# Later operand sums, no w_q checks beside the first products, more checks in the last blocks, and another order of part products

## The chip, the cores and the metric

The kernel runs on one core of one Trainium2 chip. The metric is the device time of one execution in microseconds (us), median of several executions. Five engines work side by side, each through its own instructions in a fixed order: TensorE (PE, matrix products), VectorE (DVE), ScalarE (ACT), GpSimd (POOL) and SyncE (SP, which here issues nearly all transfers between the chip's memory and the core).

## The reference

For x of 2048 tokens by 512 numbers, the output is x plus two branches of the layer-normed x, called xn here.

```python
# branch A: real part of a 2-D Fourier transform
a = einsum("bsd,ed->bse", xn, dft_hid_re); b = einsum("bsd,ed->bse", xn, dft_hid_im)
y = einsum("ts,bse->bte", dft_seq_re, a) - einsum("ts,bse->bte", dft_seq_im, b)
# branch B: 32 heads of product-key experts
q = einsum("nd,dhc->nhc", xf, w_q); q1, q2 = q[..., :128], q[..., 128:]
s1 = einsum("nhd,ed->nhe", q1, k1); s2 = einsum("nhd,ed->nhe", q2, k2)
i1, i2 = the 2 best of 64 in s1, s2; t1, t2 = their scores
cand = t1[:, None] + t2[None, :]; eidx = i1 * 64 + i2      # 2 x 2 candidates
top_s, top_e = the 2 best candidates; g = softmax(top_s)
act = gelu(einsum("nd,nhkd->nhk", xf, u[top_e]))           # u, v: 4096 x 512
out = einsum("nhk,nhk,nhkd->nd", g, act, v[top_e])
```

## The kernel before

The tokens are 16 blocks of 128. Branch A takes the first 116 us and is not touched. Branch B is `part_b`, in two halves.

**Scores.** There are 128 steps: 8 chunks of heads by 16 token blocks. A step is 12 products on PE (`s_mm`, L252) into one bank of PSUM, a scaled copy to SBUF by ACT (L951, tiles `ss<chunk>_<block>`, four buffers), and on DVE a search for the best two of 64 for each head (MAX8 L955, FIND_INDEX8 L959). After the last block of a chunk its routing (L884 to L924: candidate sums, softmax weights `g`, packed indices `z`) is done by POOL, DVE and ACT in pieces set beside later steps. A list, `todo`, names the other work of each step. To it belong: `fill_uv` (ACT L780 and L781, POOL L782), which splits a 512 KB piece of u or v into a rounded half-precision part and the rest; `sum_u` and `sum_x`, which make the sums of operands that a Strassen-like product needs. `sum_x(b, part)` serves the pair of token blocks b, b+1. Its part 0 runs on POOL (L822 to L831: a copy of one element that orders it behind a score step, one 1024-wide subtraction L823, four 256-wide sums), its part 1 splits the result (`split4`: ACT L794, POOL L795), its part 2 stores it. As scratch it borrows two neighbouring v tiles, `v<n>` and `v<n+1>`, before those are filled with v itself. The six pairs begin at blocks 2, 4, 6, 8, 10 and 12.

**Products.** Then come 16 `z` stages (x times u, all 4096 experts, gelu) and 16 `v` stages (masked weights times v). The order is written out in `phases`: z0, z1, v0; six rounds of a z pair (b, b+1), v(b-1), v(b); then z14, v13, z15, v14, v15. A stage has 8 column groups, a pair 16. A single z stage runs a column group as 48 products (L1095) into one of four banks, which ACT empties with the gelu (L1102). A pair runs 8 of its 16 groups plainly, `c` in the order below, two blocks to a product, and the other 8 in two quads, `a` and `b`, with seven products in place of eight: `1a` is operation 1 of quad a. Each operation takes 24 products (L1164); results stay in banks X, Y and Z until all parts are added, and ACT and DVE carry the parts (L1191 to L1214). X of a quad is freed by the gelu L1191 that follows operation 4.

Beside the products the weights of the next block are built: `g_mm` (G; DVE L1242, L1247 and L1250 make one-hot masks L and R, PE L1252 multiplies them) and `w_part` (W; DVE L1260 takes gelu output times g from PSUM, ACT L1267 rounds it to a half, DVE L1268 keeps the rest).

Third, the kernel checks itself: 68 units `U` compare stored transform matrices with inputs (`compare`, `compare_w`: one load, several DVE operations, an ACT sum of magnitudes L1373 or L1418), 35 units `F[0]` are `fit` on w_q or on v pieces that are not resident (a 512 KB load at L1424 or 256 KB at L1431, then a sum of magnitudes on ACT at L1425 or L1432), and units `F[1]` do the same on resident pieces (L1436). All of these tiles and the w tiles of W turn in one pool tag, `"w"`, with four buffers. `step` runs a unit: first it issues the ACT sums that are waiting, all but the newest, then the next unit's load.

`put(phase, column group, ...)` fills the table `plan`, which says what runs behind which column group. These lines are what the change rewrites:

```python
for ph in phases[:3]:                          # z0, z1, v0
    for cg in range(1, 9, 2):
        put(ph, cg, F[0])
for ph in phases[3:]:
    if ph[0] == "z":
        for cg in (8,) if len(ph) == 3 else (1, 4):
            put(ph, cg, F[0])
        for cg in range(7, 17, 2) if len(ph) == 3 else ():
            put(ph, cg, U)
```

A list scheduler turns the program into a fixed order for each engine from its own estimates of durations, so an edit at one place moves the neighbours too.

Of the kernel before, what the change touches and what calls it, by code (L numbers as in the profile page):

```python
# [29 lines left out]
V1 = 5  # L30
# [6 lines left out]
def tile_fnet_peer(ctx, tc, x, ca, cb, c5, wt, wf, wr, wq, kt, ut, vn, out):  # L37
# [683 lines left out]
    def part_b(safe, stS, stP, stQ, stE, xt, u_sb, cmp_p, w4):  # L721
# [93 lines left out]

        def sum_x(b, part, at=None):

            n = (0, 2, 4, 4, 7, 5)[PAIRS.index(b)]
            f, t4 = scratch(n), scratch(n + 1)
            if part == 0:  # L820
                v = xq[b // 2]
                nc.gpsimd.tensor_copy(f[:, 0:1], behind(one, at))  # L822
                nc.gpsimd.tensor_tensor(f.rearrange("p (q f) -> p q f", q=2),  # L823
                                        v[:, :, 0].rearrange("p q k n -> p q (k n)"),
                                        v[:, :, 1].rearrange("p q k n -> p q (k n)"), op=ALU.add)
                b11, b21, b12, b22 = [f[:, k * 256:k * 256 + 256] for k in range(4)]
                r = [t4[:, k * 256:k * 256 + 256] for k in range(4)]
                nc.gpsimd.tensor_tensor(r[0], b12, b11, op=ALU.subtract)
                nc.gpsimd.tensor_tensor(r[1], b22, r[0], op=ALU.subtract)
                nc.gpsimd.tensor_tensor(r[2], b22, b12, op=ALU.subtract)  # L830
                nc.gpsimd.tensor_tensor(r[3], b21, r[1], op=ALU.subtract)  # L831
                return
            split4(part - 1, t4, f.bitcast(F16)[:, 0:2 * D],
                   lambda i: t_d[b // 2, :, i * 2 * D:i * 2 * D + 2 * D], at)
# [154 lines left out]
        fills = [divmod(n, 16) for n in (0, 1, 2, 8, 3, 10, 16, 4, 12, 14, 17, 5, 9, 11, 18, 6, 13, 15, 19, 7, 20,  # L989
                                         21, 22, 23, 24)]  # L990
        slots = [29, 31, 36, 43, 45] + [16 * j + i for j in range(3, 7) for i in (4, 6, 11, 13)]
        slots += [115 + 2 * n for n in range(len(fills) - len(slots))]
        assert fills[slots.index(115)] == (1, V1)
        for (which, g), n in zip(fills, slots):
            todo[n].append(lambda at, w=which, g=g: fill_uv(w, g, at))
            todo[n - (3 if n < 115 else 1)].append(lambda at, w=which, g=g: fill_load(w, g))
            if which == 0 and not safe and any(g in q for q in QUADS):
                todo[n + 5].append(lambda at, g=g: (sum_u(g, 1, at), sum_u(g, 2)))
        if not safe:
            for n, b in zip((19, 22, 25, 102, 106, 108), PAIRS):  # L1000
                todo[n].append(lambda at, b=b: sum_x(b, 0, at))
                todo[n + 5].append(lambda at, b=b: (sum_x(b, 1, at), sum_x(b, 2)))
        for g, n in zip(range(V2, 16), (25, 38, 41, 57, 73, 89, 105)):
            todo[n].append(lambda at, g=g: stage_v(g, at, False))
            todo[n - 3].append(lambda at, g=g: fill_load(1, g))
# [98 lines left out]
        if not safe:  # L1104
            sx = stE.enter_context(tc.tile_pool(name="sx", bufs=1, side="left"))
            x4 = sx.tile([P, 2, 4, 2, P], F16, name="x4")
            PLAIN = [g for g in range(16) if not any(g in q for q in QUADS)]
            SEQ = [o if o == "c" else o + q for q in "ab" for o in "152c6c3c7c4"]
            OPS = {"1": (0, None, None, 0), "2": (1, None, None, 1), "5": (None, 0, 0, None), "6": (None, 1, 1, None),
                   "3": (None, 3, None, 3), "7": (None, 2, 2, None), "4": (3, None, 3, None)}  # L1110

# [59 lines left out]
        def z_pair(b, n, after):  # L1171

            cgs = iter(PLAIN)
            st = {}
            total, done, cg = sum(2616 if o == "c" else 1344 for o in SEQ), 0, 0
            for o in SEQ:
                if o == "c":
                    u_part(b, next(cgs))
                    done += 2616
                else:  # L1180
                    op, qd = o[0], ("ab".index(o[1]) + n) % 2
                    quad = QUADS[qd]

                    def dst(a, c):
                        return ACT[b[c]][:, 2 * quad[0] + a:2 * quad[3] + 2:2 * (quad[1] - quad[0]), :]

                    def v(p):
                        return p.rearrange("p (t n) -> p t n", t=4)

                    def gelu(d, src=None):  # L1190
                        nc.scalar.activation(d, d if src is None else src, AF.Gelu_apprx_tanh, scale=zsc)  # L1191

                    if op in "125":
                        st["X" if op == "1" else "Y" if op == "2" else "Z"] = take(f"z{op}_{b[0]}_{qd}")
                    (X, Xt), (Y, Yt), (Z, Zt) = [st.get(k, (None, None)) for k in "XYZ"]
                    slot(op, quad, Z if op in "53" else Y if op == "2" else X, qd)
                    if op == "1":
                        nc.scalar.activation(dst(0, 0), v(X), AF.Copy)
                    elif op == "2":
                        nc.vector.tensor_tensor(dst(0, 0), v(Y), dst(0, 0), op=ALU.add)  # L1200
                        banks.append(Yt)
                    elif op == "5":
                        nc.scalar.activation(dst(1, 0), v(Z), AF.Copy)
                    elif op == "6":
                        nc.scalar.activation(dst(0, 1), v(X), AF.Copy)
                        gelu(dst(0, 0))
                    elif op == "3":
                        nc.vector.tensor_tensor(dst(0, 1), v(Z), dst(0, 1), op=ALU.add)
                        banks.append(Zt)
                    elif op == "7":  # L1210
                        nc.scalar.activation(dst(1, 1), v(X), AF.Copy)
                        nc.vector.tensor_tensor(dst(1, 1), dst(1, 1), dst(1, 0), op=ALU.add)
                        gelu(dst(0, 1))
                    else:  # L1214
                        gelu(dst(1, 0), v(X))
                        gelu(dst(1, 1))
                        banks.append(Xt)
                    done += 1344
                while cg < 16 and done * 16 >= (cg + 1) * total:
                    after(cg)  # L1220
                    cg += 1
# [276 lines left out]
        def take(name):  # L1498
            tag = banks.pop(0)
            return psz.tile([P, 512], F32, tag=tag, name=name), tag  # L1500
# [56 lines left out]
        for b in range(14):  # L1557
            put(("v", b), 3, lambda b=b: compact_d(b + 2))
        if not safe:
            for ph in phases[:3]:  # L1560
                for cg in range(1, 9, 2):
                    put(ph, cg, F[0])
            for ph in phases[3:]:
                if ph[0] == "z":
                    for cg in (8,) if len(ph) == 3 else (1, 4):
                        put(ph, cg, F[0])
                    for cg in range(7, 17, 2) if len(ph) == 3 else ():
                        put(ph, cg, U)
                elif ph[1] < 14:
                    for cg, f in enumerate((None, F[1], F[1], None, U, U, U, F[0]) if ph[1] % 2 == 0 else (  # L1570
# [2 lines left out]
                            put(ph, cg, f)  # L1573
            for cg in range(3):
                put(("v", 14), cg, F[1])
                put(("v", 15), cg, F[1])
            for f, n in ((U, 68), (F[0], NK + 16 - V2), (F[1], 16 + V2)):
                assert sum(v.count(f) for v in plan.values()) >= n
# [188 lines left out]
```

## Time and profile before

| what | value |
|---|---|
| median of 3 runs | 1156.5 us (1153.89 to 1159.17) |
| the profiled execution, its own time | 1156.79 us |
| its span in the trace | 1154.7 us |
| PE busy | 1123.6 us, 97% of the span |
| DVE busy | 952.2 us, 82% |
| ACT busy | 642.1 us, 56% |
| POOL busy | 314.5 us, 27% |
| mean granted TensorE clock | 0.994 of full |

The span is what the trace covers; the 2.1 us between it and the execution's time lie outside the trace. The stages stand in the trace so: branch A up to 116 us, scores up to 419.69, z0 to 443.8, z1 to 480.86, v0 after it, the pairs from about 500 to 1031, then z14, v13, z15, v14 and v15; the last product ends at 1147.9. Timeline rows read: start, duration, engine, line, operation, output<-input with shapes, how many in a row, and in brackets the idle time of that engine just before, with what ended it. A waits row reads: engine and line that waited <- what ended the wait: us in total, times, longest.

### The profile page before, as it was taken

How to read it: one execution, taken by the hardware profiler on the slowest of the kernel's cores; microseconds unless marked ns; L12 is line 12 of the kernel's file. 1: busy time of each engine (PE TensorE's matmuls, PEld its weight loads, DVE VectorE, ACT ScalarE, POOL GpSimd, SP SyncE). 2: the span in 40 equal slices, each digit the busy share in tenths (PEclk: the TensorE clock that was granted, in tenths of full speed). 3: DMA queues.
4: the chain of work that ended last, by engine and by line, in shares of the span. 5: the costliest groups of instructions: out<-in, count | busy, mean ns of one | idle time of the engine just before them, and what ended most of it. 6: DMA issues, size and time to landing. Idle time of an engine off the chain costs nothing.

```text
span 1154.7 us, 27307 instructions
## 1 busy us (share of the span) xinstructions
PE 1123.6 (97%) x10748; PEld 726.8 (63%) x10748; DVE 952.2 (82%) x2855; ACT 642.1 (56%) x1086; POOL 314.5 (27%) x342
## 2 busy tenths in 40 slices
PE   9999999999999896999999999999999999999997
PEld 6455554544544366769579479569569568658763
DVE  7899979989888896894996897898987887888570
ACT  6557598788786554555436535535535535533440
POOL 1425996788789710000010010010010010000000
PEclk9999999999999999899999999999999999999999
DMA  9983554534433206663764664654665655452423
GB/s 290 289 208 137 169 193 153 172 102 164 158 98 111 92 15 237 208 242 106 238 203 154 224 206 175 226 198 169 223 204 185 222 193 196 156 175 73 130 74 104
DMA packets 114856, 198.36 MB, mean 172 GB/s; under 512 B 34068, under 2 KB 57499, under 8 KB 114718
## 3 DMA queue, kind: packets, MB, share of 16 engines
q1 hardware_dynamic: 114416, 196.45, 51.0%
q8 instruction: 86, 1.41, 0.5%
q14 instruction: 52, 0.43, 0.1%
q10 hardware_dynamic: 302, 0.08, 0.0%
HBM read 165.75 MB, written 24.97 MB: 165 GB/s over the span
## 4 chain that ended last, share of the span: by engine, by line
PE 74%; DVE 13%; DMA 6%; ACT 2%; POOL 2%; issue 1%; SPq 1%; DVEq 0%; ACTq 0%; POOLq 0%
PE v L1297 26%; PE s L252 21%; PE z L1095 13%; PE z L1164 8%; PE g L1252 4%; DMA fit<-in_wq_dram 3%; DVE vals L955 2%; PE m L148 1%; DVE u L955 1%; DVE idx L959 1%; DVE u L959 1%; DVE L L1242 1%; PE p L449 1%; DMA s<-s_d 1%; DVE w L1260 1%
## 5 line engine op out<-in xcount | busy, mean ns | idle before, releaser
L252 PE MATMUL s<-m,xq 128*128 128x512 f16 x1344 | 297.6, 379 | 3.8 <-ACT ss L951 3.5
L1297 PE MATMUL v<-v,act 128*128 128x512 f16 x1056 | 233.2, 379 | 0.0
L252 PEld LDWEIGHTS <-xq 128*128 128x128 f16 x1344 | 129.8, 98 | 155.2 <-issue 5.6
L1095 PE MATMUL z<-xb,u 128*128 128x128 f16 (+1 forms) x2688 | 223.3, 243 | 2.1 <-ACT act L1102 1.6
L1095 PEld LDWEIGHTS <-u 128*128 128x128 f16 x2688 | 198.8, 99 | 15.0 <-issue 2.4
L1242 DVE TENSOR_TENSOR L<-io_lam,cmp 128x2048 f16<-128x2048 f16 x128 | 159.3, 1244 | 56.3 <-PE g L1252 56.3
L1310 POOL TENSOR_TENSOR y<-y,xr 128x512 f32<-128x512 f32 x15 | 27.0, 1802 | 614.4 <-DMA y<-y_d 284.9
L1297 PEld LDWEIGHTS <-act 128*128 128x128 f16 x1056 | 101.2, 98 | 117.5
L955 DVE MAX8 vals<-ss 128x8 f32<-128x64 f32 x896 | 133.4, 216 | 7.0 <-ACT ss L951 7.0
L951 ACT ACTIVATE ss<-s,wsc 128x512 f32<-128x512 f32 x120 | 81.6, 684 | 45.3 <-PE s L252 30.6
L1297 PE MATMUL v<-v,w 128*128 128x512 f16 x480 | 106.2, 379 | 0.0
L959 DVE FIND_INDEX8 idx<-vals,ss 128x8 uint16<-128x256 f32 x224 | 93.8, 419 | 0.0
L1267 ACT ACTIVATE act<-w 128x1024 f16<-128x1024 f32 x36 | 48.3, 1358 | 73.0 <-DVE w L1260 72.6
L1373 ACT ACTIVATE cx<-cx 128x896 f32<-128x896 f32 x64 | 60.6, 947 | 43.8 <-DVE cx L1353 30.2
L1297 PEld LDWEIGHTS <-w 128*128 128x128 f16 x480 | 46.0, 98 | 53.3
L1252 PEld LDWEIGHTS <-L 128*128 128x128 f16 x2048 | 60.6, 96 | 21.2 <-issue 10.8
L1252 PE MATMUL g<-R,L 128*128 128x32 f16 x2048 | 62.1, 176 | 10.1 <-DVE R L1250 6.2
L1260 DVE SCALAR_TENSOR_TENSOR w<-act,scl,g 128x1024 f32<-128x1024 f32 x44 | 55.9, 1278 | 18.4 <-DMA fit<-in_wq_dram 9.7
L1102 ACT ACTIVATE act<-z,scl 128x256 f32<-128x256 f32 (+1 forms) x88 | 43.9, 525 | 42.2 <-PE z L1095 42.1
L1268 DVE TENSOR_TENSOR act<-w,act 128x1024 f16<-128x1024 f32 x44 | 60.5, 1378 | 3.8 <-ACT act L1267 3.7
L1164 PEld LDWEIGHTS <-s 128*128 128x128 f16 x1080 | 62.7, 98 | 0.5
L1347 DVE TENSOR_TENSOR cx<-cx 128x512 f32<-128x512 f32 (+2 forms) x84 | 48.6, 608 | 15.3 <-DMA cx<-in_cb_dram 15.0
(363 smaller groups left out, 1725.4 us busy)
## 6 DMA issues: line engine op xcount, KB each, us to landing
v<-v_d SPq DMA_DIRECT2D x67, 512.0 KB, 4.6
cx<-in_cb_dram SPq DMA_DIRECT2D x64, 448.0 KB, 5.5
s<-s_d SPq DMA_DIRECT2D x35, 512.0 KB, 3.6
w<-in_wq_dram SPq DMA_DIRECT2D x28, 512.0 KB, 5.4
fit<-in_wq_dram SPq DMA_DIRECT2D x28, 512.0 KB, 5.5
uv<-in_vn_dram SPq DMA_DIRECT2D x16, 512.0 KB, 3.8
uv<-in_ut_dram SPq DMA_DIRECT2D x16, 512.0 KB, 4.0
c<-in_ca_dram SPq DMA_DIRECT2D x8, 512.0 KB, 7.7
```

The source lines that it names most:

```text
L252: nc.tensor.matmul(ps, xt[i][:, l, kd, :], m[:, r, kd, :], start=(n == 0), stop=(n == 3 * KD - 1))
L951: nc.scalar.activation(s, ps, AF.Copy, scale=inv)
L955: nc.vector.max(vals[:, i, w, :, h], s[:, g, :])
L959: nc.vector.max_index(idx[:, i, w].rearrange("p k h -> p (k h)"), vals[:, i, w, 0:2].rearrange("p k h -> p (k h)"), s[:, w * HC:g + 1, :]. ...
L1095: nc.tensor.matmul(ps if n == 1 else ps.rearrange("p (b n) -> p b n", b=2), ug[:, l, c % 2, kd, :], xb2[:, k0, r, kd, :] if n == 1 else xb ...
L1164: nc.tensor.matmul(bank[:, t * P:(t + 1) * P], lt, rt, start=(t == k == 0 and op in "125"), stop=(t == 3 and k == 5), skip_group_check=op ...
L1242: nc.vector.tensor_tensor(L.rearrange("p t (l two) -> p t l two", two=2), io_lam.rearrange("p (l two) -> p l two", two=2).unsqueeze(1).to_ ...
L1252: nc.tensor.matmul(p[:, hf, t * NC:(t + 1) * NC], L[:, t, :], R[:, t, :], start=True, stop=True)
L1260: nc.vector.scalar_tensor_tensor(w, act[:, :, ts], fw, p.rearrange("p h (n c) -> p c (h n)", c=NC), op0=ALU.mult, op1=ALU.mult)
L1268: nc.vector.tensor_tensor(w16[..., 1], w, w16[..., 0], op=ALU.subtract)
L1297: nc.tensor.matmul(pv, w16[:, c, :, l], v_sb[g][:, r, cc, :], start=(n + cc == 0 and k == 0), stop=(n == 15 and cc == 1 and k == 2))
L1373: later.append(lambda: nc.scalar.activation(tf[:, P:], tf[:, P:], AF.Abs, accum_out=chk[:, n:n + 1]))
```

## The change

Four edits, all in `part_b`.

1. `sum_x` of pair 8 takes tiles v5 and v6 as scratch in place of v4 and v5. The last three `sum_x` start at steps 107, 111 and 114 (before 102, 106 and 108), and their second part comes 5, 5 and 4 steps later. The last four fills move from steps 115, 117, 119, 121 to 119, 121, 123, 125.
2. In a pair, the four operations 4a, 1b, 5b, 2b change order: before `4a 1b 5b 2b`, now `1b 5b 4a 2b`; at the end `c 7b c 4b` becomes `7b c c 4b`. The books on the banks are kept by quad, since quad b now begins before quad a has ended.
3. The w_q checks beside z0 and z1 (four each) go; the four beside v0 stay. New ones stand at v12, v13 and twice at v14, and two more in each of z14 and z15.
4. A pair now has three compare units (groups 9, 12, 15) in place of five (7, 9, 11, 13, 15); z14 and z15 have four each and v14 three, where there were none.

The number of checks that run is the same, 68 and 35.

```diff
-            n = (0, 2, 4, 4, 7, 5)[PAIRS.index(b)]
+            n = (0, 2, 4, 5, 7, 5)[PAIRS.index(b)]
...
-        slots += [115 + 2 * n for n in range(len(fills) - len(slots))]
+        slots += [119 + 2 * n for n in range(len(fills) - len(slots))]
...
-            todo[n - (3 if n < 115 else 1)].append(lambda at, w=which, g=g: fill_load(w, g))
+            todo[n - (3 if n < 119 else 1)].append(lambda at, w=which, g=g: fill_load(w, g))
...
-            for n, b in zip((19, 22, 25, 102, 106, 108), PAIRS):
+            for n, b in zip((19, 22, 25, 107, 111, 114), PAIRS):
                 todo[n].append(lambda at, b=b: sum_x(b, 0, at))
-                todo[n + 5].append(lambda at, b=b: (sum_x(b, 1, at), sum_x(b, 2)))
+                todo[n + (4 if n == 114 else 5)].append(lambda at, b=b: (sum_x(b, 1, at), sum_x(b, 2)))
...
-            SEQ = [o if o == "c" else o + q for q in "ab" for o in "152c6c3c7c4"]
+            SEQ = "1a 5a 2a c 6a c 3a c 7a c 1b 5b 4a 2b c 6b c 3b 7b c c 4b".split()
...
-                        st["X" if op == "1" else "Y" if op == "2" else "Z"] = take(f"z{op}_{b[0]}_{qd}")
-                    (X, Xt), (Y, Yt), (Z, Zt) = [st.get(k, (None, None)) for k in "XYZ"]
+                        st[o[1], "X" if op == "1" else "Y" if op == "2" else "Z"] = take(f"z{op}_{b[0]}_{qd}")
+                    (X, Xt), (Y, Yt), (Z, Zt) = [st.get((o[1], k), (None, None)) for k in "XYZ"]
...
-            for ph in phases[:3]:
-                for cg in range(1, 9, 2):
-                    put(ph, cg, F[0])
+            for cg in (1, 3, 5, 7):
+                put(("v", 0), cg, F[0])
+            for ph, cg in ((("v", 12), 0), (("v", 13), 3), (("v", 14), 3), (("v", 14), 7)):
+                put(ph, cg, F[0])
             for ph in phases[3:]:
                 if ph[0] == "z":
-                    for cg in (8,) if len(ph) == 3 else (1, 4):
+                    for cg in (8,) if len(ph) == 3 else (1, 3, 4, 5):
                         put(ph, cg, F[0])
-                    for cg in range(7, 17, 2) if len(ph) == 3 else ():
+                    for cg in (9, 12, 15) if len(ph) == 3 else (0, 2, 3, 6):
                         put(ph, cg, U)
...
             for cg in range(3):
                 put(("v", 14), cg, F[1])
+                put(("v", 14), cg + 4, U)
```

The order of the engines shows what this moves. First POOL near the end of the scores; `v4_919 <- xq4` is the sum for pair 8, `v7 <- xq5` that for pair 10, L795 the end of a split, `v3`, `u7` and `v4` at L782 are fills. Before:

```order
L822 COPY v4_919<-ss6_6_4788 128x1
L823 TENSOR_TENSOR v4_919<-xq4_107 128x1024
L828 TENSOR_TENSOR v5_920<-v4_919 128x256
L830 TENSOR_TENSOR v5_920<-v4_919 128x256
L829 TENSOR_TENSOR v5_920<-v4_919,v5_920 128x256
L831 TENSOR_TENSOR v5_920<-v4_919,v5_920 128x256
L782 TENSOR_TENSOR v3_918<-uv1_3_4660,v3_918 128x1024
L795 TENSOR_TENSOR v7_922<-v7_922,v6_921 128x1024
L851 TENSOR_TENSOR uv1_15_4811<-uv1_15_4811,vh15_4930 128x1024
L822 COPY v7_922<-ss6_10_4947 128x1
L823 TENSOR_TENSOR v7_922<-xq5_108 128x1024
L828 TENSOR_TENSOR v8_923<-v7_922 128x256
```

Now:

```order
L782 TENSOR_TENSOR v3_918<-uv1_3_4660,v3_918 128x1024
L795 TENSOR_TENSOR v7_922<-v7_922,v6_921 128x1024
L851 TENSOR_TENSOR uv1_15_4804<-uv1_15_4804,vh15_4923 128x1024
L822 COPY v5_920<-ss6_11_4967 128x1
L823 TENSOR_TENSOR v5_920<-xq4_107 128x1024
L828 TENSOR_TENSOR v6_921<-v5_920 128x256
L830 TENSOR_TENSOR v6_921<-v5_920 128x256
L829 TENSOR_TENSOR v6_921<-v5_920,v6_921 128x256
L831 TENSOR_TENSOR v6_921<-v5_920,v6_921 128x256
L782 TENSOR_TENSOR u7_134<-uv0_7_4882,u7_134 128x1024
L782 TENSOR_TENSOR v4_919<-uv1_4_4952,v4_919 128x1024
L822 COPY v7_922<-ss6_15_5084 128x1
```

The sum of pair 8 stood ahead of the fill of v3, in v4 and v5, and the next sum right behind L851; now the sum of pair 8 stands there, in v5 and v6, and the fills of u7 and v4 come ahead of the next sum.

Second, ACT from the last gelus of z0 (`act0`) to the second weight tile of block 0, through the beginning of z1 (`act1`); `fit` are w_q checks. Before:

```order
L1102 ACTIVATE act0_5697<-z0_5_5978,scl_93 128x512
L1102 ACTIVATE act0_5697<-z0_6_6070,scl_93 128x512
L1425 ACTIVATE fit0_5824,sums_87<-fit0_5824 128x1024
L1425 ACTIVATE fit1_5926,sums_87<-fit1_5926 128x1024
L1102 ACTIVATE act0_5697<-z0_7_6120,scl_93 128x512
L1425 ACTIVATE fit2_6068,sums_87<-fit2_6068 128x1024
L1425 ACTIVATE fit3_6210,sums_87<-fit3_6210 128x1024
L1267 ACTIVATE act0_5697<-w0_0_6262 128x32x32
L1102 ACTIVATE act1_5698<-z1_0_6212,scl_93 128x512
L1267 ACTIVATE act0_5697<-w0_1_6369 128x32x32
```

Now:

```order
L1102 ACTIVATE act0_5697<-z0_5_5974,scl_93 128x512
L1102 ACTIVATE act0_5697<-z0_6_6063,scl_93 128x512
L1102 ACTIVATE act0_5697<-z0_7_6113,scl_93 128x512
L1267 ACTIVATE act0_5697<-w0_0_6252 128x32x32
L1102 ACTIVATE act1_5698<-z1_0_6202,scl_93 128x512
L1267 ACTIVATE act0_5697<-w0_1_6356 128x32x32
```

The four sums of magnitudes that stood ahead of `w0_0` and of the first gelu of z1 are gone; the gelus and weight roundings keep their order.

Third, ACT in the middle of a pair, here blocks 6 and 7; `z6_3` is a plain column group, `z1_6_0` is bank X of quad a, `z1_6_1` and `z5_6_1` are X and Z of quad b. Before:

```order
L1373 ACTIVATE cx22_9906,sums_87<-cx22_9906 128x896
L1211 ACTIVATE act7_9559<-z1_6_0_9560 128x4x128
L1191 ACTIVATE act7_9559<-act7_9559,scl_93 128x4x128
L1373 ACTIVATE cx23_10063,sums_87<-cx23_10063 128x896
L1102 ACTIVATE act6_9558<-z6_3_9848,scl_93 128x256
L1102 ACTIVATE act7_9559<-z6_3_9848,scl_93 128x256
L1373 ACTIVATE cx24_10124,sums_87<-cx24_10124 128x896
L1191 ACTIVATE act6_9558<-z1_6_0_9560,scl_93 128x4x128
L1198 ACTIVATE act6_9558<-z1_6_1_9913 128x4x128
L1373 ACTIVATE cx25_10253,sums_87<-cx25_10253 128x896
L1203 ACTIVATE act6_9558<-z5_6_1_9939 128x4x128
```

Now:

```order
L1373 ACTIVATE cx18_10001,sums_87<-cx18_10001 128x896
L1211 ACTIVATE act7_9505<-z1_6_0_9506 128x4x128
L1191 ACTIVATE act7_9505<-act7_9505,scl_93 128x4x128
L1373 ACTIVATE cx19_10154,sums_87<-cx19_10154 128x896
L1102 ACTIVATE act6_9504<-z6_3_9794,scl_93 128x256
L1102 ACTIVATE act7_9505<-z6_3_9794,scl_93 128x256
L1373 ACTIVATE cx20_10241,sums_87<-cx20_10241 128x896
L1198 ACTIVATE act6_9504<-z1_6_1_9825 128x4x128
L1203 ACTIVATE act6_9504<-z5_6_1_9851 128x4x128
L1191 ACTIVATE act6_9504<-z1_6_0_9506,scl_93 128x4x128
```

The gelu that empties X of quad a (`act6 <- z1_6_0`, L1191) stood ahead of the first copies of quad b (L1198, L1203); now it comes behind both.

More of the change, by code (lines that the diff above doesn't have):

```diff
@@ L991, in part_b @@
         slots = [29, 31, 36, 43, 45] + [16 * j + i for j in range(3, 7) for i in (4, 6, 11, 13)]
-        slots += [115 + 2 * n for n in range(len(fills) - len(slots))]
-        assert fills[slots.index(115)] == (1, V1)
+        slots += [119 + 2 * n for n in range(len(fills) - len(slots))]
+        assert fills[slots.index(119)] == (1, V1)
         for (which, g), n in zip(fills, slots):
             todo[n].append(lambda at, w=which, g=g: fill_uv(w, g, at))
-            todo[n - (3 if n < 115 else 1)].append(lambda at, w=which, g=g: fill_load(w, g))
+            todo[n - (3 if n < 119 else 1)].append(lambda at, w=which, g=g: fill_load(w, g))
             if which == 0 and not safe and any(g in q for q in QUADS):
```

## The prediction

> **What bounds the kernel now.** I read the page's busy shares first.
>
> ```profile
> PE 1123.6 (97%) x10748; PEld 726.8 (63%) x10748; DVE 952.2 (82%) x2855; ACT 642.1 (56%) x1086; POOL 314.5 (27%) x342
> ```
>
> PE sets the time. The change alters no product, so only PE's 31 us without work (1154.7 - 1123.6) can shrink, and new gaps can open. The table of busy time by stretch says where those 31 us lie (start and end, length, then PE, PEld, DVE, ACT, POOL, granted clock, DMA share, GB/s).
>
> ```profile
> 353.00:397.00 44.00, 41.93 (x216) 19.26 (x213) 34.88 (x185) 28.89 (x46) 38.81 (x43) 1.00 0.36 120
> 397.00:443.00 46.00, 42.98 (x500) 30.96 (x499) 45.52 (x237) 22.45 (x32) 6.39 (x3) 1.00 0.16 47
> 443.00:500.00 57.00, 47.05 (x702) 37.28 (x700) 42.34 (x53) 28.98 (x41) 1.27 (x1) 0.91 0.67 236
> 500.00:549.00 49.00, 48.50 (x628) 42.35 (x626) 30.85 (x72) 25.36 (x50) 2.09 (x1) 1.00 0.49 172
> 899.00:990.00 91.00, 88.55 (x988) 63.35 (x986) 72.96 (x122) 43.77 (x78) 4.48 (x2) 1.00 0.56 190
> 1031.00:1155.00 124.00, 116.74 (x1392) 80.47 (x1389) 74.08 (x136) 39.18 (x61) 5.03 (x4) 0.98 0.28 91
> ```
>
> The late scores and z0 (353 to 443) have 5.1 us of PE idle, with DVE at 45.52 of 46 in their second half: there the binding engine is DVE. z1 and v0 (443 to 500) have 10.0, at a clock of 0.91. The last pair has 2.5, and the tail 7.3, nearly all of it behind the last product. Third, what PE waited for, over the whole span:
>
> ```profile
> PE g L1252 <- DVE R L1250: 6.2, 3, 5.8
> PE g L1252 <- DVE w L1260: 3.8, 1, 3.8
> PE s L252 <- ACT ss L951: 3.5, 3, 2.1
> PE z L1164 <- ACT act L1211: 3.5, 2, 2.5
> PE z L1095 <- ACT act L1102: 1.6, 2, 0.9
> PE z L1164 <- ACT w L1211: 0.6, 1, 0.6
> PE z L1095 <- DVE w L1200: 0.5, 1, 0.5
> ```
>
> Each part of the change aims at some of these rows.
>
> **The w_q checks beside z0 and z1.** PE's timeline, from the end of z0 to the start of v0:
>
> ```profile
> 438.47 5.52 PE L1095 MATMUL z<-xb,u 128*128 128x128 f16 x96
> 443.83 0.95 PE L1252 MATMUL g<-R,L 128*128 128x32 f16 x32
> 444.63 8.20 PE L1095 MATMUL z<-xb,u 128*128 128x128 f16 x144
> 456.64 0.55 PE L1252 MATMUL g<-R,L 128*128 128x32 f16 x16 [3.81 <-DVE w L1260]
> 463.03 0.59 PE L1252 MATMUL g<-R,L 128*128 128x32 f16 x16 [5.84 <-DVE R L1250]
> 463.46 7.52 PE L1095 MATMUL z<-xb,u 128*128 128x128 f16 x96
> 480.86 2.53 PE L1297 MATMUL v<-v,act 128*128 128x512 f16 x11
> ```
>
> The waits are put down to DVE, but DVE itself had been held. First ACT's rows, then DVE's:
>
> ```profile
> 452.38 1.06 ACT L1425 ACTIVATE fit<-fit 128x1024 f32<-128x1024 f32 x1 [10.34 <-DMA fit<-in_wq_dram]
> 454.54 0.67 ACT L1102 ACTIVATE act<-z,scl 128x512 f32<-128x512 f32 x1
> ```
>
> ```profile
> 455.31 1.28 DVE L1260 SCALAR_TENSOR_TENSOR w<-act,scl,g 128x1024 f32<-128x1024 f32 x1 [9.66 <-DMA fit<-in_wq_dram]
> ```
>
> ACT stood 10.34 us at a check's sum of magnitudes, waiting for its load. Queued behind it was the last gelu of z0 (454.54), though z0's products had ended by 443.83; behind that gelu stood DVE's first weight tile (455.31), whose PSUM reading frees the bank for PE's g at 456.64; behind the tile the masks for the g at 463.03. The wait did a second thing:
>
> ```profile
> 450.00:460.00 10.00, 3.38 (x67) 3.19 (x65) 4.18 (x5) 6.81 (x12) 0.00 (x0) 0.87 0.84 326
> 460.00:470.00 10.00, 6.97 (x98) 6.97 (x98) 9.64 (x13) 6.52 (x10) 0.00 (x0) 0.62 1.01 333
> ```
>
> The granted clock fell to 0.62, and the 96 products at 463.46 took 7.52 where those at 438.47 took 5.52: 2.0 us. So of the 37.03 us from 443.83 to 480.86, 3.81 + 5.84 + 2.0 = 11.65 hang on the checks. In the new order no check stands between the end of z0 and v0 on ACT, so the gelu runs right behind z0 and the chain starts some 10 us sooner. What is late next is DVE: from 443 to 500 it has 42.34 us of work and PE 47.05 - 2.0 = 45, nearly level, and in the stretch from 397 to 443, where DVE is full, PE loses 3.0 of 46. The most is the whole 11.65; the least takes 3.0 for such coupling and as much as half of it again, which leaves 7. I take 10.5, nearer the top since PE still has more work than DVE: **-10.5 (-11.65 to -7)**. The four checks beside v0 stay as they were.
>
> **The late sums of x.** Where DVE lost time near the scores' end:
>
> ```profile
> 373.66 1.15 ACT L780 ACTIVATE v<-uv,ss 128x1024 f16<-128x1024 f32 x1 [6.20 <-POOL v L795]
> ```
>
> ```profile
> 376.60 0.74 DVE L955 MAX8 vals<-ss 128x8 f32<-128x64 f32 x5 [4.65 <-ACT ss L951]
> ```
>
> The fill of v4 on ACT waited 6.20 us for POOL to finish the split of pair 8, whose scratch was v4. ACT's score evictions stood behind it, and DVE, the binding engine of this stretch, stood 4.65. Scratch v5 and v6 takes that wait away: at most -4.65, and PE's own idle caps it at 5.1. What it triggers: the sum of pair 12 now lies on POOL ahead of routing's multiplication g (L895), and DVE's conversion of g, in line ahead of the score searches, waits for it.
>
> ```profile
> 376.06 2.12 POOL L823 TENSOR_TENSOR v<-xq 128x1024 f32<-128x1024 f16 x1
> 378.26 0.73 POOL L828 TENSOR_TENSOR v<-v 128x256 f32<-128x256 f32 x1
> ```
>
> One sum is 2.12 + 4 x 0.73 = 5.0 us, less what DVE has to do meanwhile. That may cost 1 to 5; against it stands other POOL backlog that no longer delays the routing's start. The ends are -4.65 and +2; I take **-3**, as the wait that goes is certain and the new one is partly covered. The fills, six or eight steps later, have POOL nearly idle from 397 on (6.39 of 46) and lie beside z0; nothing in z0 reads the last v tiles.
>
> **The order in a pair.** The loads of the checks cost the pairs too. One row of ACT and one of PE, last pair:
>
> ```profile
> 963.35 1.06 ACT L1425 ACTIVATE fit<-fit 128x1024 f32<-128x1024 f32 x1 [3.03 <-DMA fit<-in_wq_dram]
> ```
>
> ```profile
> 966.70 1.50 PE L1164 MATMUL z<-x,u 128*128 128x128 f16 x24 [2.45 <-ACT act L1211]
> ```
>
> A check held ACT, L1211 came late, and operation 4a waited 2.45. With 4a two operations later (two times about 1.35 us between starts) this cover is enough for most: the three rows of waits above that name L1211 and L1200 give 3.5 + 0.6 + 0.5 = 4.6 us, and all may go. But 4a now ends only one operation, 2b, ahead of the column group that takes its bank. The same place in pair 6, ACT and then PE:
>
> ```profile
> 704.54 0.68 ACT L1191 ACTIVATE act<-z,scl 128x512 f32<-128x512 f32 x1
> 705.11 0.60 ACT L1198 ACTIVATE act<-z 128x512 f32<-128x512 f32 x1
> ```
>
> ```profile
> 705.27 2.78 PE L1095 MATMUL z<-xb,u 128*128 128x256 f16 x24
> ```
>
> The gelu that empties the bank ended at 705.22, and the group started at 705.27, so the bank is already just in time. In the new order this gelu comes behind L1198 and L1203, two times 0.60; ACT has little slack there. I put 1.0 a pair, 0 to 1.5, for six pairs 6 (0 to 9), and 1 (0 to 3) for the first pair, whose first compare unit's load now follows two checks'. Sum: 7 - 4.6 = **+2.4 (-4.6 to +7.4)**. Two units fewer in each pair relieve DVE (72.96 of 91), which is not what PE waits for there: nothing.
>
> **The tail.** z14 and z15 each get two more checks and four compare units, v14 three units and two checks. DVE has 50 us free in the last 124, ACT 85, so the work itself fits. What counts is the order on ACT: four sums of magnitudes, each waiting for a load, now stand between z14's gelus. Before, three such waits in the tail were
>
> ```profile
> ACT fit L1432 <- DMA fit<-v_d: 7.3, 3, 3.2
> ```
>
> with no cost to PE. Four w_q loads of twice the size may hold ACT up to 3.2 each; a gelu may be late by about one column group before PE lacks a bank. The bounds are 0 and 6; I take **+2**, since the transfers are at a share of 0.28 here. The checks' verdict, due before the end of v15, is behind v14's last units and should stay ahead of the last product.
>
> **The sum**: 1156.8 (this execution) - 10.5 - 3 + 2.4 + 2 = 1147.7. The execution stands 0.3 above the median of the runs, so about **1147.5**, 0.8% faster. With its terms' bounds not all at one end, this case spans 1141 to 1154.
>
> **The rivals.**
> *The pairs eat the gain.* At the upper bound, with the bank late by 1.5 in every pair and the tail at its 6: -13.5 + 7.4 + 6 leaves 1157 (no change); with the pairs alone, 1153. For it: the just-in-time row at 705.27. Against: the list of waits shows ACT at ease in most pairs. Chance 0.14.
> *More is gained.* The bank comes in time, the tail costs nothing: -10.5 - 3 - 4.6 gives 1139. Chance 0.15.
> *The stall moves to z14 and z15: slower.* Mechanism: a w_q load comes more than about 10 us after ACT reaches its sum, the gelus and the first weight tile of the next block queue up as at 452.38, and PE loses 11.65 in each of the two stages: 1147.7 - 2 + 23.3 = 1169. It decides from loads as late as z1's 10.34; a load then competed with DMA shares of 0.84 to 1.01, against 0.28 in the tail, and four of z1's loads were started in one burst. Chance 0.08.
> *POOL and DVE get in each other's way* in the late routing. A row of POOL, then two of DVE:
>
> ```profile
> 394.20 2.13 POOL L782 TENSOR_TENSOR v<-uv,v 128x1024 f16<-128x1024 f32 x1
> ```
>
> ```profile
> 394.36 2.12 DVE L897 TENSOR_TENSOR z<-g,z 128x128 f16<-128x128 f32 x1
> 437.52 0.25 DVE L897 TENSOR_TENSOR z<-g,z 128x96 f16<-128x96 f32 x1
> ```
>
> The same instruction takes 2.12 beside POOL's fill and 0.25 with POOL idle (there over 96 in place of 128 columns). With two more sums beside the routing, four or five such DVE instructions could pay 1.9 each: 8 to 9 in place of -3, hence 1147.5 + 12 = 1159.5, no better than before. Chance 0.04. The Trainium skill, "SBUF — State Buffer", section "Who interferes with whom", says that the second of a VectorE and a GpSimd instruction on the shared ports is blocked until the first ends; the pair of rows agrees (2.12 beside 2.13).
> *The checks were not the cause:* z1 waits for another load or for DVE just as long; 1147.5 + 10.5 = 1158. Against it, the row at 443.83 shows PE and the gelu's input ready. Chance 0.03.
>
> **Chances.** The forecast has 0.56. A measurement of this kernel tells about 0.5% (5.8 us) from no change. Faster by more (below 1150.7): most of the forecast's case and all of the larger gain, 0.65; within: the forecast's upper end, the pairs' case, the ports and the checks' case, 0.25; slower: the stall in the tail and what I have overlooked, 0.10. The range from 1139 to 1157 takes in the larger gain and the pairs' case.
>
> **What would show it.** Right: no PE wait above 1 us between z0 and v0, clock 1.00 there, z0's end to v0's start 25 to 28 us; no ACT fill waiting for L795 near the scores' end; no waits at L1211 in the pairs, but new small ones of the column group behind 2b on the gelu L1191; PE idle of a few us in z14. Wrong: PE waits in z14 or z15 as long as z1's, a DVE wait on POOL's L895 above 5, or several us of PE idle in each pair.

## The result

Six runs of the changed kernel have a median of 1147.52 us (1145.57 to 1148.88), six runs of the kernel before 1157.76. The ratio is 0.9912, with a 95% interval of 0.9891 to 0.9934: 0.9% faster, against 0.8% forecast. The profiled execution took 1145.57 us, with a span of 1143.8, 10.9 less than before. What PE waited for in its whole span, in the rows that belong to branch B (engine and line, releaser: total us, times, longest):

```profile
PE z L1095 <- ACT act L1191: 4.7, 4, 1.8
PE s L252 <- ACT ss L951: 2.5, 1, 2.5
PE g L1252 <- DVE R L1250: 0.9, 3, 0.3
PE z L1164 <- ACT act L1102: 0.5, 1, 0.5
PE z L1164 <- ACT w L1102: 0.5, 1, 0.5
PE z L1095 <- ACT w L1191: 0.3, 1, 0.3
```

The 9.7 us at L1252 are gone but for small rests, and so are all waits on L1211. In their place the row on top is new. PE's timeline from the end of z0 to the start of v0, in the changed kernel:

```profile
442.05 0.95 PE L1252 MATMUL g<-R,L 128*128 128x32 f16 x32
442.85 8.20 PE L1095 MATMUL z<-xb,u 128*128 128x128 f16 x144
450.89 0.95 PE L1252 MATMUL g<-R,L 128*128 128x32 f16 x32
451.69 5.52 PE L1095 MATMUL z<-xb,u 128*128 128x128 f16 x96
457.05 0.95 PE L1252 MATMUL g<-R,L 128*128 128x32 f16 x32
467.09 2.54 PE L1297 MATMUL v<-v,act 128*128 128x512 f16 x11
```

There is no bracket left, and the 96 products take 5.52 us. The busy time by stretch (PE, PEld, DVE, ACT, POOL, clock, DMA share, GB/s), for z1 and for the tail from z14 on:

```profile
442.00:467.00 25.00, 25.00 (x529) 25.00 (x527) 22.57 (x27) 11.78 (x14) 1.28 (x1) 1.00 0.63 204
1022.00:1143.00 121.00, 113.70 (x1377) 78.93 (x1375) 86.87 (x186) 56.15 (x95) 3.73 (x4) 0.99 0.51 167
```

PE is busy through all of z1 at full clock with DVE at 22.57 of 25; the tail, 3 us shorter here, has 12.8 us more work on DVE and 17 more on ACT than the last stretch of before.

To see where the 10.9 us came from, take PE's timeline and subtract the start of each stage's first product from that of the next stage, in one profile each:

| stretch | before | changed | difference |
|---|---|---|---|
| to the start of z0 | 419.69 | 419.81 | +0.1 |
| z0 | 24.14 | 22.24 | -1.9 |
| z1 | 37.03 | 25.04 | -12.0 |
| six pairs together | 257.88 | 259.31 | +1.4 |
| the v stages from v0 to v12 | 296.50 | 296.38 | -0.1 |
| z14, v13, z15, v14, v15 | 112.65 | 113.58 | +0.9 |
| behind the last product | 6.81 | 7.44 | +0.6 |

The first row hides two things. Branch A, which no edit touches, ends 1.4 us later in the changed kernel's profile (one and the same score step starts at 117.68 against 116.31); the scores behind it take 1.25 us less.

### The profile page after: what moved, and what is told of

The parts are those of the page before. It is cut to its first block, busy times and chain, and to the rows that moved or that the text cites. A ratio compares the mean times of both kernels' runs of the same rounds, so it can differ in the third digit from the quotient of the medians.

```text
span 1143.8 us, 27323 instructions
## 1 busy us (share of the span) xinstructions
PE 1123.1 (98%) x10748; PEld 726.1 (63%) x10748; DVE 949.7 (83%) x2855; ACT 642.1 (56%) x1086; POOL 312.3 (27%) x342
## 4 chain that ended last, share of the span: by engine, by line
PE 50%; DVE 7%; DMA 5%; POOL 2%; ACT 2%; issue 1%; SPq 0%; ACTq 0%; POOLq 0%; DVEq 0%
PE v L1297 24%; PE z L1095 14%; PE z L1164 7%; DMA cx<-in_cb_dram 4%; PE g L1252 4%; PE s L252 2%; DVE L L1242 1%; DVE w L1260 1%; DVE cx L1347 1%; DVE act L1268 1%; ACT cx L1373 1%; POOL v L823 1%; DMA fit<-in_wq_dram 1%; DVE R L1247 0%; DVE R L1250 0%
## 5 line engine op out<-in xcount | busy, mean ns | idle before, releaser
L252 PE MATMUL s<-m,xq 128*128 128x512 f16 x1344 | 297.4, 379 | 2.5 <-ACT ss L951 2.5
L252 PEld LDWEIGHTS <-xq 128*128 128x128 f16 x1344 | 129.7, 98 | 153.5 <-issue 3.8
L1095 PE MATMUL z<-xb,u 128*128 128x128 f16 (+1 forms) x2688 | 219.9, 242 | 5.0 <-ACT act L1191 4.7
L1310 POOL TENSOR_TENSOR y<-y,xr 128x512 f32<-128x512 f32 x15 | 24.6, 1643 | 638.8 <-DMA y<-y_d 380.5
L1252 PEld LDWEIGHTS <-L 128*128 128x128 f16 x2048 | 60.2, 96 | 12.0 <-issue 1.5
L1260 DVE SCALAR_TENSOR_TENSOR w<-act,scl,g 128x1024 f32<-128x1024 f32 x44 | 55.7, 1276 | 13.4 <-ACT act L1191 13.4
L1252 PE MATMUL g<-R,L 128*128 128x32 f16 x2048 | 62.0, 176 | 1.0 <-DVE R L1250 0.9
```

The costliest lines, as they stand in the source:

```text
L252: nc.tensor.matmul(ps, xt[i][:, l, kd, :], m[:, r, kd, :], start=(n == 0), stop=(n == 3 * KD - 1))
L1095: nc.tensor.matmul(ps if n == 1 else ps.rearrange("p (b n) -> p b n", b=2), ug[:, l, c % 2, kd, :], xb2[:, k0, r, kd, :] if n == 1 else xb ...
L1252: nc.tensor.matmul(p[:, hf, t * NC:(t + 1) * NC], L[:, t, :], R[:, t, :], start=True, stop=True)
L1260: nc.vector.scalar_tensor_tensor(w, act[:, :, ts], fw, p.rearrange("p h (n c) -> p c (h n)", c=NC), op0=ALU.mult, op1=ALU.mult)
```

## The experiments

### Each edit alone

Four kernels each apply one of the four edits to the kernel before; their diffs are those of the change, cut apart and shown in part (`...` stands for lines left out). The late sums alone:

```diff
-            n = (0, 2, 4, 4, 7, 5)[PAIRS.index(b)]
+            n = (0, 2, 4, 5, 7, 5)[PAIRS.index(b)]
...
-        slots += [115 + 2 * n for n in range(len(fills) - len(slots))]
+        slots += [119 + 2 * n for n in range(len(fills) - len(slots))]
...
-            for n, b in zip((19, 22, 25, 102, 106, 108), PAIRS):
+            for n, b in zip((19, 22, 25, 107, 111, 114), PAIRS):
...
```

> The kernel before with the first edit alone (late sums of x and late fills). My theory: the fill of v4 no longer waits for the split of pair 8, DVE loses one long wait near the scores' end and gets a shorter one on POOL's L895 (2 to 3 us); z0 ends about 1.9 us sooner, and z1 still has its stall of 37 us, so the time falls by about 2 us (ratio 0.998). Rival: z0's gain in the changed kernel comes from the checks that left z0, then this kernel shows none.

The moved w_q checks alone:

```diff
-            for ph in phases[:3]:
-                for cg in range(1, 9, 2):
-                    put(ph, cg, F[0])
+            for cg in (1, 3, 5, 7):
+                put(("v", 0), cg, F[0])
+            for ph, cg in ((("v", 12), 0), (("v", 13), 3), (("v", 14), 3), (("v", 14), 7)):
+                put(ph, cg, F[0])
...
-                    for cg in (8,) if len(ph) == 3 else (1, 4):
+                    for cg in (8,) if len(ph) == 3 else (1, 3, 4, 5):
```

> The kernel before with the third edit alone (w_q checks away from z0 and z1, eight put into the last blocks). My theory: z1 falls from 37.0 to about 25 us and the clock stays at 1.00 there; the last blocks pay 0 to 2 us for the checks; the time falls by 9 to 12 us (ratio 0.990 to 0.992). Rival: without the late sums the scores' end holds z1 up in another way, then z1 stays above 28 us and the gain is below 8 us.

The order of the part products alone:

```diff
-            SEQ = [o if o == "c" else o + q for q in "ab" for o in "152c6c3c7c4"]
+            SEQ = "1a 5a 2a c 6a c 3a c 7a c 1b 5b 4a 2b c 6b c 3b 7b c c 4b".split()
...
```

> The kernel before with the second edit alone (order of part products in a pair). My theory: the waits of operation 4a (4.6 us in all) go and waits of the column group behind 2b on the gelu L1191 come, about 1 us in most pairs, so the six pairs change by -2 to +2 us together (ratio 0.998 to 1.002). Rival: the new waits come from the moved compare units and not from the order, then the pairs gain 4 to 5 us here (ratio 0.996).

The moved compare units alone:

```diff
-                    for cg in range(7, 17, 2) if len(ph) == 3 else ():
+                    for cg in (9, 12, 15) if len(ph) == 3 else (0, 2, 3, 6):
                         put(ph, cg, U)
...
+                put(("v", 14), cg + 4, U)
```

> The kernel before with the fourth edit alone (three compare units in a pair in place of five, eleven in z14, z15 and v14). My theory: PE does not wait for DVE's checks in the pairs, so the pairs change by less than 2 us together and the last blocks by less than 1.5 us: ratio 0.998 to 1.002. Rival: fewer units free ACT for the sums behind 4a, then the 4.6 us of waits shrink to half or less (ratio 0.997 to 0.998).

Measured against the kernel before (1157.64 us in this set):

| edit alone | median, us | ratio, 95% interval | six pairs, us | z0 and z1, us |
|---|---|---|---|---|
| late sums | 1153.14 | 0.9969 (0.995 to 0.9987) | 256.79 | 55.51 |
| w_q checks | 1143.79 | 0.9886 (0.9853 to 0.9918) | 255.34 | 49.20 |
| order of part products | 1167.77 | 1.0112 (1.0075 to 1.0148) | 266.90 | 61.02 |
| compare units | 1153.19 | 0.9962 (0.9945 to 0.9979) | 253.85 | 60.17 |
| before | 1157.64 | 1 | 257.88 | 61.17 |
| all four | 1147.52 | 0.9912 (0.9891 to 0.9934) | 259.31 | 47.28 |

The moved checks alone have a lower ratio than the whole change, which was measured in another set, but the two intervals overlap. The column of the pairs has to be read with care: six kernels whose edits leave the plan of the pairs as it was (before, late sums, w_q checks and the three of the next two sections) spread from 255.2 to 258.4 us, so differences of up to some 3 us are not told from none.

The order of part products makes the kernel 1.1% slower: +9.0 us in the pairs, where -2 to +2 was expected. Its rival, that the moved units bring the new waits, fell. In ACT's timeline of that kernel, second pair (blocks 4 and 5), the sum of a compare unit waits for DVE, and the gelu that frees quad a's bank stands behind it; the PE row below shows who pays:

```profile
617.49 0.95 ACT L1373 ACTIVATE cx<-cx 128x896 f32<-128x896 f32 x1 [0.95 <-DVE cx L1353]
618.35 0.19 ACT L1373 ACTIVATION_READ_ACCUMULATOR cx<-cx 128x1 f32 x1
618.44 0.67 ACT L1191 ACTIVATE act<-z,scl 128x512 f32<-128x512 f32 x1
```

```profile
619.16 4.10 PE L1095 MATMUL z<-xb,u 128*128 128x256 f16 x24 [2.97 <-ACT act L1191]
```

The copies L1198 and L1203 are not the whole delay. Call lead the time from the end of 4a, the last to write the bank, to the operation that takes the bank again: with one operation of lead, the sums of checks between 4a and this gelu count here too.

The compare units alone gain 4.0 us in the pairs, where the forecast had nothing and this run's own rival had the waits of 4a shrink to half or less. No wait on L1211 remains there. The largest part, 2.6 us, lies in the last pair (44.72 to 42.12), and there the cause shows on SP, where the order of issues has moved. The check's load was issued, before,

```profile
956.35 0.43 SPq L1424 DMA_DIRECT2D fit<-in_wq_dram  x1
```

and its sum waited until 963.35 on ACT, as quoted in the prediction. With two units fewer, from the same place in SP's and in ACT's timelines:

```profile
953.36 0.42 SPq L1424 DMA_DIRECT2D fit<-in_wq_dram  x1
```

```profile
959.33 1.06 ACT L1425 ACTIVATE fit<-fit 128x1024 f32<-128x1024 f32 x1 [2.07 <-DMA fit<-in_wq_dram]
```

The load leaves 3.0 us sooner and the sum runs 4.0 sooner, early enough for L1211. Some 1.1 of the 3.0 are the two transfers of a compare unit that stood just ahead of the load; for the rest, the issues ahead of those come sooner too. So in this pair the units held PE through SP's queue and not through DVE, which was where the forecast had looked; in the six kernels of the spread above the last pair took 43.8 to 44.7 us. The other five pairs together changed by 1.4, within that spread.

The late sums alone give 3.6 us by the ratio; the 2 that was expected lies inside its interval (1.5 to 5.8 us). In the profile z0 and z1 together are 5.7 us shorter: 1.9 of it is z0, and 3.0 are a shorter stall in z1 (its two waits are 1.88 and 4.82). z0 began 1.5 later in this profile, so v0 starts 4.1 sooner. That fits the checks' loads, which left 3.1 us sooner. First SP's timeline and one row of its waits in the kernel before, then its timeline with the late sums:

```profile
437.80 0.38 SPq L1052 DMA_DIRECT2D z_d<-z  x1
443.85 1.77 SPq L1288 DMA_DIRECT2D v<-v_d  x3
445.66 2.03 SPq L1424 DMA_DIRECT2D fit<-in_wq_dram  x4
```

```profile
SPq L1288 <- DMA z_d<-z: 5.4, 1, 5.4
```

```profile
435.41 0.38 SPq L1052 DMA_DIRECT2D z_d<-z  x1
441.27 1.28 SPq L1288 DMA_DIRECT2D v<-v_d  x3
442.60 2.02 SPq L1424 DMA_DIRECT2D fit<-in_wq_dram  x4
```

The order of issue is the same: the store of the packed indices z, then, when it has landed, three loads of v and the four checks. The late sums let DVE finish the routing 2.4 us sooner, and so the store and all behind it leave earlier. The end of z0 is not what the loads wait for: with the late sums it comes at 443.48, behind their issue. With the checks gone that part has nothing left to give: z0 and z1 take 49.20 us with the checks' edit alone, 47.28 with all four.

### Why the checks held z1: ACT's queue or the shared buffers

Two kernels take one cause away each. The first keeps the loads of the first eight checks and leaves out their sums:

```diff
-                later.append(lambda: nc.scalar.activation(t, t, AF.Abs, accum_out=fits[:, n:n + 1]))
+                if n > 7:
+                    later.append(lambda: nc.scalar.activation(t, t, AF.Abs, accum_out=fits[:, n:n + 1]))
+                else:
+                    later.append(lambda: None)
...
```

> The kernel before, but the eight checks beside z0, z1 and early v0 keep only their loads: their sums of magnitudes on ACT are left out, and the results of eight other checks stand in their place. It separates ACT's queue from the shared buffers. If ACT's queue alone made the stall of z1, z1 falls to 25 to 27 us. If the loads hold the four buffers that the first weight tile needs, the tile still waits for the first load to land (about 452 us in before), and z1 stays at 33 to 36 us.

Its ACT and DVE timelines:

```profile
442.70 0.69 ACT L1102 ACTIVATE act<-z,scl 128x512 f32<-128x512 f32 x1 [1.99 <-PE z L1095]
453.10 1.35 ACT L1267 ACTIVATE act<-w 128x1024 f16<-128x1024 f32 x1 [9.71 <-DVE w L1260]
```

```profile
451.78 1.28 DVE L1260 SCALAR_TENSOR_TENSOR w<-act,scl,g 128x1024 f32<-128x1024 f32 x1 [7.47 <-DMA fit<-in_wq_dram]
```

The last gelu of z0 runs at 442.70, right behind its products, and the first weight tile still waits until 451.78: all four buffers of the tag are filled by checks, and the tile needs one whose load has landed. z1 takes 35.4 us (442.50 to 477.93).

The second kernel does the reverse: two checks beside z0 and none beside z1, so two buffers stay free, but two sums stand on ACT ahead of the gelu.

```diff
-            for ph in phases[:3]:
-                for cg in range(1, 9, 2):
-                    put(ph, cg, F[0])
+            for cg in (1, 3):
+                put(("z", 0), cg, F[0])
+            for cg in (1, 3, 5, 7):
+                put(("v", 0), cg, F[0])
...
```

> The kernel before with only the first two checks beside z0 (none beside z1; the others where the third edit puts them). Two of the four buffers stay free for the first weight tiles, but the two sums still stand ahead of the last gelu of z0 on ACT. After the run without sums, which showed that the held buffers alone make nearly the whole stall, this one asks of ACT's queue alone. If it alone is enough too, z1 stays at 31 to 36 us; if the buffers were the only cause, z1 is 25 to 27 us.

```profile
451.73 1.06 ACT L1425 ACTIVATE fit<-fit 128x1024 f32<-128x1024 f32 x1 [11.17 <-DMA fit<-in_wq_dram]
453.88 0.67 ACT L1102 ACTIVATE act<-z,scl 128x512 f32<-128x512 f32 x1
```

Here the gelu is late, at 453.88, and z1 takes 37.6 us (442.35 to 479.97). Either cause is enough by itself. Two checks cost as much as eight, and taking away only the sums, or only some of the held buffers, gains 1.6 us in z1 or nothing. Both kernels ran once; it is their traces that tell.

### Why the loads came late

> The kernel before with the first four w_q loads issued from POOL's queue, so that they no longer stand on SP behind the store of z and three loads of v. If the lateness of the issue (445.66 us) is the root, they land before z0 ends, and z1 is 25 to 29 us with all eight checks in place. If the landing itself takes that long, or the buffers' memory is free only at the end of z0, z1 stays above 33 us.

```diff
-                nc.sync.dma_start(t.rearrange("p (h k) -> p h k", h=2), wq[1 + n // 4, n % 4 // 2, n % 2])
+                (nc.gpsimd if n < 4 else nc.sync).dma_start(t.rearrange("p (h k) -> p h k", h=2), wq[1 + n // 4, n % 4 // 2, n % 2])
```

In POOL's timeline the issue is no earlier, and the view of the tile gives the time to landing (least, median, most):

```profile
446.00 1.93 POOL L1424 DMA_DIRECT2D fit<-in_wq_dram  x3 [32.70 <-issue]
```

```profile
DMA to landing us min/median/max: 7.2/8.9/11.7
```

POOL had nothing else to do for 32.70 us and still issued at 446.00. So SP's queue does not set the start; what releases POOL then the profile does not name. It comes 0.7 us after SP's own first load behind the store of z (issued at 439.12, loads of v from 445.28). The program says why this may be: `z` lies in the pool `sp`, which is closed right behind this store, and the pool of the four buffers opens on the same side of SBUF after it. That the buffers lie in memory which the scores hold until z is stored fits every run here, and the end of z0 was excluded above; for POOL's queue it is argued and not shown. The first check's sum ran 8.3 us after its issue (446.00 to 454.27), against 6.7 in the kernel before (445.66 to 452.38), but SP now issued other loads of 512 KB in the same microseconds, so the run does not tell whether POOL's way is slower. It took 1165.37 us, a single run. Of the ways tried, only putting the checks elsewhere freed z1.

### The order of part products, mended

The changed kernel with the old order:

> The changed kernel with the old order of part products (edits 1, 3 and 4 without 2). My theory after the first runs: the new order alone cost the pairs 9 us, the fewer units alone saved them 4; without the new order the waits of the column group on L1191 (5.0 us) go and those of operation 4a do not come back, so the pairs together fall from 259.3 to 253 to 255 us and the kernel is 4 to 6 us faster than the changed one: ratio to before 0.985 to 0.988. Rival: edit 2 is needed once the units have moved, then this kernel is as slow as the changed one (0.991) or slower.

With a column group moved ahead of 2b, which by its own time gives 4a's bank 2.6 us in place of 1.3 before it is taken again:

```diff
-            SEQ = "1a 5a 2a c 6a c 3a c 7a c 1b 5b 4a 2b c 6b c 3b 7b c c 4b".split()
+            SEQ = "1a 5a 2a c 6a c 3a c 7a c 1b 5b 4a c 2b 6b c 3b 7b c c 4b".split()
```

> The changed kernel with one plain column group moved ahead of 2b (1b 5b 4a c 2b 6b in place of 1b 5b 4a 2b c 6b). If the cost of the order lies in the one operation of lead between 4a and the taking of its bank, this lead is now 2.6 us in place of 1.3 and the waits on L1191 fall from 5.0 to under 1.5 us: pairs at 254 to 256 us, ratio 0.986 to 0.989. Rival: 2b, not the column group, then waits on L1191 as long as before, no change (0.991).

With 4a one operation sooner:

```diff
-            SEQ = "1a 5a 2a c 6a c 3a c 7a c 1b 5b 4a 2b c 6b c 3b 7b c c 4b".split()
+            SEQ = "1a 5a 2a c 6a c 3a c 7a c 1b 4a 5b 2b c 6b c 3b 7b c c 4b".split()
```

> The changed kernel with 4a one operation sooner (1b 4a 5b 2b). By the same theory the lead is two operations, 2.7 us, and 4a has one operation less of cover against L1211: waits on L1191 under 2 us, at 4a under 1.5 us, ratio 0.986 to 0.989. Rival: the waits lie in ACT's own queue however the products stand, then the pairs stay at 259 us (0.991).

| changed kernel, but | median, us | ratio to before, 95% interval | six pairs, us |
|---|---|---|---|
| old order | 1141.71 | 0.9863 (0.9833 to 0.9892) | 252.38 |
| column group ahead of 2b | 1141.35 | 0.9866 (0.9835 to 0.9898) | 252.48 |
| 4a one operation sooner | 1144.38 | 0.9885 (0.9855 to 0.9915) | 256.74 |

Once the units have moved, the old order has no stall left to cure: its only wait of this kind is

```profile
PE z L1164 <- ACT w L1211: 0.2, 1, 0.2
```

The order of the change costs 6.9 us in the pairs (259.31 - 252.38), and with the column group ahead of 2b this cost vanishes. Two operations of lead, 2.7 us, do less: waits on L1191 of 0.5 to 1.5 us stay. The two leads are less alike than planned. In PE's timeline the column group brings the products of G with it, in the third pair:

```profile
685.76 1.50 PE L1164 MATMUL z<-x,u 128*128 128x128 f16 x24
687.10 2.78 PE L1095 MATMUL z<-xb,u 128*128 128x256 f16 x24
689.72 0.95 PE L1252 MATMUL g<-R,L 128*128 128x32 f16 x32
690.52 1.50 PE L1164 MATMUL z<-xb,u 128*128 128x128 f16 x24
```

4a is the first row and 2b the last, so the lead is 3.4 us (687.10 to 690.52). That fits the difference; no run separates it from the changed order on ACT.

### The new wait near the scores' end

The forecast's new wait on POOL's L895 came. The first rows are POOL's, the last is DVE's, in the changed kernel:

```profile
392.53 0.72 POOL L831 TENSOR_TENSOR v<-v,v 128x256 f32<-128x256 f32 x1
393.21 0.32 POOL L895 TENSOR_TENSOR g<-c,g 128x64 f32<-128x64 f32 x1
393.49 2.13 POOL L795 TENSOR_TENSOR v<-v,v 128x1024 f16<-128x1024 f32 x1
```

```profile
393.57 2.13 DVE L896 CAST z<-g 128x128 f16<-128x128 f32 x1 [2.38 <-POOL g L895]
```

DVE waits 2.38 us, and then its conversion takes 2.13 beside POOL's L795. A last kernel adds one edit to the one with the column group ahead of 2b:

```diff
-                ge.tensor_tensor(g[:, :, 1, :], ex, g[:, :, 0, :], op=ALU.mult)
+                (nc.vector if j == NCH - 2 else ge).tensor_tensor(g[:, :, 1, :], ex, g[:, :, 0, :], op=ALU.mult)
```

> The changed kernel with the column group ahead of 2b and with the multiplication of g of the last but one chunk on DVE in place of POOL, so that DVE's conversion does not wait behind a sum (2.4 us). If that wait sets PE's wait of 2.46 us near the scores' end, the time falls by 1 to 2.5 us against the version without this edit: ratio to before 0.984 to 0.986. Rival: the scores' end is set by DVE's total work, no change (0.9866).

It took 1138.83 us, ratio 0.9835 (0.9797 to 0.9874), in a set where the kernel before took 1156.66. DVE's wait is gone, and PE's row at L252 shrinks from 2.5 to

```profile
PE s L252 <- ACT ss L951: 0.6, 1, 0.6
```

z0 starts at 416.57 us, against 418.23 without this edit. The trace shows the 1.7 us; the intervals of the two ratios overlap, so the total does not, and the pairs took 254.01 us here against 252.48, which gives most of it back in this profile. This kernel has the lowest ratio of all, with PE busy 99% of its span, but it is not told apart from the first two rows of the table above.

## Why the prediction was right

The forecast of 1147.5 us met the median of 1147.52, but that close a hit is luck. The kernel before moved to 1157.76 in the larger set, so the gain was 10.2 us where 9.0 had been forecast; in the two profiles the steps add up to -10.9 where the sum had -9.1. By the steps:

**The w_q checks** were set at -10.5 and gave -12.0, slightly more than the bound of 11.65. No coupling to DVE appeared (22.57 busy of 25). The chain named, sums of magnitudes, gelu, weight tile, is real, but only half of the cause: the four shared buffers alone hold z1 nearly as long (35.4 us against 37.0). DVE's row at L1260 with its wait of 9.66 us put down to the load of `fit` said so, and I read it as ACT's delay handed on. Since the change takes both away the sum did not suffer.

**The late sums** were set at -3 and gave -1.9 in z0 and, with branch A's 1.4 taken out, -1.25 in the scores. The wait on L780 shrank to 1.6 us, and the new one on L895 came at 2.4 us, inside its 1 to 5. What the forecast did not have is that the store of z leaves sooner with them; alone, they shorten z1's stall that way.

**The pairs** were set at +2.4 and gave +1.4, by two wrong terms that cancel: luck again, and within the spread of the pairs. "Two units fewer in each pair relieve DVE (72.96 of 91), which is not what PE waits there for: nothing" failed: the units alone gave -4.0, in the last pair through the loads on SP ahead of ACT's sums. And the new order was priced at 7 - 4.6; alone it costs 9.0, and beside the moved units 6.9, because the old order's stalls go with the units and the order has nothing left to save. Without the order the pairs take 5.5 us less than before (252.38), and with it +6.9 on top: that is the +1.4. Each edit was costed against before, and not against a kernel with the other edits in it.

**The tail** was set at +2 and gave +0.9 in the stages and +0.6 behind the last product. The four sums between z14's gelus found their loads landed, with waits of 1.2 us at the most, and the PE idle of a few us in z14 did not come; the verdict came in time.

Of the rivals, "the pairs eat the gain" is nearest to what the order does: 5.0 us of waits on L1191 in four long and one short piece. "The stall moves to z14 and z15" did not happen. POOL and DVE did collide (2.13 us at L896), within the gain of the sums.

## What to carry to other kernels

Where an engine's wait is put down to a transfer that it does not read, look for a shared buffer: a queue and a buffer pool can each hold the same chain, and taking one of them away then gains little or nothing. Cost an edit in the kernel that the other edits leave, and not in the kernel before; an order meant to save a stall is a loss once another edit has removed the stall. A forecast that fits in total still needs its terms measured apart: here they led to a kernel that is 1.6% faster than the one before, where the change had given 0.9%.

## What was not expected of the hardware

DVE's conversion of 128 numbers a partition (L896) took 2.13 us beside a POOL instruction of 2.13, though it has a single input. In the kernel before, the same chunk's took 0.34 us; but six of its seven conversions of this shape took 1.28 to 2.14 us, each beside a POOL instruction of 2.1 us and ending with it, so the change moved the stretch to this chunk and did not bring it. The score searches (MAX8, FIND_INDEX8) show no such stretch beside POOL's work: none of them takes more than 0.24 and 0.43 us in the whole trace.
